# Turning the gate's rows of two chunks with one transfer, and a smaller block of zeros

## The chip, the cores and the metric

The kernel runs on one core of a Trainium2 chip. The metric is device time in microseconds (us). TensorE multiplies matrices, VectorE and ScalarE work on tiles in the on-chip memory (SBUF), GpSimd issues indirect transfers, and SyncE (SP) issues all other transfers, one after the other, from one queue. The transfers themselves run on 16 DMA engines.

## The reference, cut to what matters

Attention over 8 batches of 3072 tokens, with 256 features and keys of 64, gives `x`. A gate then sends each token to one of 8 experts (two layers, 256 to 1024 to 256); an expert takes its first 768 tokens in order, and all other tokens give zeros.

```python
scores = (1.0 / S) * np.matmul(z, z.transpose(0, 2, 1))
attn = np.maximum(scores, 0.0) ** 2
x = (u * np.matmul(attn, v)).reshape(B * S, D)
logits = x @ w_gate
expert_idx = np.argmax(logits, axis=1)
# softmax weight of the chosen expert; disp[e] = its first `capacity` tokens
h = np.maximum(np.einsum('ecd,edf->ecf', disp, w1), 0.0)
y = np.einsum('ecf,efd->ecd', h, w2)
# out[i] = gate weight * y of the token's slot, or zeros for tokens beyond capacity
```

## The kernel before, in words

Every fp32 value is split into two fp16 halves, a high and a low one, and a product is three fp16 matmuls. Attention goes by blocks of 512 queries (four chunks of 128 tokens), 14 blocks in all, since by then each expert has had its 768 tokens; the last block has two chunks only. The code after the straight part, for inputs where that is not so, is skipped here. A block takes 12 pairs of key tiles. Scores are symmetric, so scores of earlier blocks are stored (`kept`, line 942) and later loaded and turned by one transfer each (`ld`, line 858); there are 40 such loads, and five buffers of them, which TensorE gives back.

When a block's sums are done, `route` (line 648 on) runs the gate on it. The rows are scaled and split: ScalarE writes the high halves (line 666), VectorE the low halves (line 669), both into a tile `xr` with one row of 264 words (1056 bytes) for each token: 256 words that hold the two halves, four with the gate's weight (line 729), four with the token's number (line 732). A transposing transfer from SyncE's queue turns the halves of one chunk, 128x512 fp16, into `xt` (line 677): 54 of them in the kernel. TensorE makes the logits out of `xt` (line 684), four matmuls a chunk, VectorE takes the largest, counts places, and GpSimd scatters each chunk's rows into the experts' buffer `disp` (line 84).

The order of all this is written at build time by a planner: `Chain` holds stages of items with an engine and an assumed cost, and `weave` emits an item when an assumed clock of its engine allows. A transposing transfer is of the kind `XB`; line 194 moves the planned clock of SyncE on by the larger of 1.2 and 0.3 plus its cost. The gate's transfers are given 0.45 each. The stage of the gate's matmuls waits in the plan for the planned landing and then 4.5 us more (`LAG`), 0.5 in the last block.

Rows of `out` that no expert fills must be zeros. `put_zeros` (line 1253) stores a block of 512 rows, 512 KB, out of a tile of zeros with 512 columns, 48 times: 14 during the last two blocks of attention, the others while the experts run. The experts read 768 rows of `disp` at a time, turned by one transfer (`fxt`, line 1120), in two buffers.

Of the kernel before, what the change touches and what calls it, by code (L numbers as in the profile page):

```python
# [9 lines left out]
F32 = mybir.dt.float32  # L10
F16 = mybir.dt.float16
I32 = mybir.dt.int32
AF = mybir.ActivationFunctionType
# [5 lines left out]
P = 128  # L19
BLK = 512  # L20
# [6 lines left out]
def attention_moe_kernel(ctx: ExitStack, tc: tile.TileContext, u, v, z, w_gate, w1, w2, out, cap):  # L27
    nc = tc.nc
    B, S, D = u.shape
    DQ = z.shape[2]  # L30
    E = w_gate.shape[1]
# [7 lines left out]
    DC = D // P  # L39
    FC = F // P  # L40
    CAPP = -(-cap // P) * P
    ROWW = D + MROW
    SLAB = min(CAPP, 768)
    NB0 = min(NBLK, -(-(E * cap * 7) // (6 * BLK)))
    assert DQ == 64 and D == 256 and S % BLK == 0 and F % P == 0 and DC * F == 2 * 1024

    const = ctx.enter_context(tc.tile_pool(name="const", bufs=1))
# [33 lines left out]
    def scatter(key, dst, idx, src, bound):  # L81


        r = nc.gpsimd.indirect_dma_start(out=dst, out_offset=bass.IndirectOffsetOnAxis(ap=idx, axis=0), in_=src,  # L84
                                         in_offset=None, bounds_check=bound, oob_is_err=False)
        if straight[0]:
            apart(r, key, [key] + (["zeros"] if cleared[0] and key == "out" else []))
            scattered[key].append(r.ins.name)
# [16 lines left out]
    cnt = const.tile([P, E], F16, name="cnt")  # L105
    wg16 = const.tile([P, DC, 2 * E], F16, name="wg16")
    wginv = const.tile([P, 1], F32, name="wginv")
    zero = const.tile([P, 512], F32, name="zero")
    more = const.tile([1, 1], I32, name="more")
    redo = const.tile([1, 1], I32, name="redo")  # L110
    short = const.tile([1, 1], I32, name="short")
# [536 lines left out]
    def route(x, bt, after, lag, cc, rid):  # L648
# [7 lines left out]
        def r_bits():  # L656
            st.rs, inv = pow2(st.m, cc, 3, "rs")
            st.f = sm.tile([P, cc], F32, tag="rf", name="rf")
            st.fg = sm.tile([P, cc], F32, tag="rfg", name="rfg")
            ts(st.f, inv, bt.cb, ALU.mult)  # L660
            ts(st.fg, inv, bt.cbg, ALU.mult)
            st.xr = sb.tile([P, cc, ROWW], F32, tag="xr", name="xr")
            st.x16 = st.xr.bitcast(F16)

        def r_hi(c):
            return lambda: nc.scalar.activation(st.x16[:, c, 0:D], st.x[:, c, :], AF.Copy, scale=st.rs[:, c:c + 1])  # L666

        def r_lo(c):
            return lambda: nc.vector.scalar_tensor_tensor(
                out=st.x16[:, c, D:2 * D], in0=st.x[:, c, :], scalar=st.rs[:, c:c + 1], in1=st.x16[:, c, 0:D],  # L670
                op0=ALU.mult, op1=ALU.subtract)

        def r_tr(c):
            def f():
                if c == 0:
                    st.xt = sb.tile([P, cc, 2 * DC, P], F16, tag="xt", name="xt", bufs=1)
                nc.sync.dma_start_transpose(out=st.xt[:, c], in_=st.x16[:, c, 0:2 * D])
            return ("XB", 0.45, f, None)

        def r_lg():  # L680
            st.lg = ps.tile([P, cc, 2, E], F32, tag="m", name="lg", bufs=1)
            for c in range(cc):
                for q in range(2 * DC):
                    nc.tensor.matmul(st.lg[:, c].rearrange("p h e -> p (h e)"), lhsT=st.xt[:, c, q, :],  # L684
                                     rhs=wg16[:, q % DC, :], start=(c == 0 and q == 0),
                                     stop=(c == cc - 1 and q == 2 * DC - 1), skip_group_check=True)

# [30 lines left out]
        def r_exp():  # L718
            nc.scalar.activation(st.ex, st.ex, AF.Exp)

        def r_gate():
            s = sm.tile([P, cc], F32, tag="es", name="es")
            g = sm.tile([P, cc], F32, tag="eg", name="eg")
            nc.vector.tensor_reduce(out=s, in_=st.ex, axis=AX.X, op=ALU.add)
            ts(s, s, 1e-9, ALU.add)
            nc.vector.reciprocal(g, s)
            nc.vector.tensor_mul(g, g, st.f)
            meta = st.xr[:, :, D:D + 8]
            nc.vector.tensor_copy(meta[:, :, 0:4], g.unsqueeze(2).to_broadcast([P, cc, 4]))

        def r_tok():
            nc.vector.tensor_copy(st.xr[:, :, D + 4:D + 8], tokid[:, 0:cc].unsqueeze(2).to_broadcast([P, cc, 4]))
            ts(tokid, tokid, float(cc * P), ALU.add)

        def r_slot():
# [15 lines left out]
            nc.vector.tensor_add(cnt, cnt, c1)  # L751

        def r_sc(c):
            return lambda: scatter("disp", disp, st.slot[:, c:c + 1], st.xr[:, c, :], E * CAPP - 1)

        def hi(h):
            return [("ACT", 0.4, r_hi(c), None) for c in (2 * h, 2 * h + 1)]
# [2 lines left out]
            return [("DVE", 0.4, r_lo(c), None) for c in (2 * h, 2 * h + 1)]  # L760

        def tr(h):
            return [r_tr(c) for c in (2 * h, 2 * h + 1)]

        nh = cc // 2
        Chain([
# [466 lines left out]
    with tc.manual_schedule():  # L1233

        halved = NB0 >= 3 and NB0 % BPB != 1
        bats = {b: batch(b) for b in range(-(-NB0 // BPB))}
        for b, bt in bats.items():
            n = min(BPB, NB0 - b * BPB)  # L1240
            bt.follows = {(j - 1, j) for j in range(1, n)}
            for i, j in ((i, j) for j in range(n) for i in range(j - 1)):
                bt.kept[i, j] = dram.tile([BLK, 2, 2, HB], F16, name=f"kept{b}_{i}_{j}")
        b0 = bats[0]
        early = min(5 * P, CAPP)
        cuts = [(0, early - P), (early - P, P)]
        assert halved
        prepare(b0, True)
        make_consts()
        warm_up(30)  # L1250
        Chain([[("DVE", 1.2, more_consts, "consts")], [("DVE", 0.8, prep_gate, "gate")]], 4, 40.0)

        def put_zeros(i):
            def f():
                r = nc.sync.dma_start(
                    out=out[i * BLK:(i + 1) * BLK].rearrange("(q r h) d -> q r (h d)", q=P, h=2),
                    in_=zero.unsqueeze(1).to_broadcast([P, BLK // P // 2, 2 * D]))
                if i >= NB0:
                    apart(r, "zeros", ["out"])
                    cleared[0] = True  # L1260
            return ("SP", 1.46, f, ("zero", i))


        zq = deque(range(NB0))

        begun = [Bag() for _ in range(1 + len(cuts))]

        def begin(after):
            for (s0, n), sx in zip(cuts, begun[1:]):
                slab(0, s0, n, sx, after, 0)  # L1270

        def hook(p):
            n, g = divmod(p, NPAIR)
            if p == 1:
                init_disp()
            b, ib = divmod(n, BPB)
            if g == 0 and ib == (b == 0) and b + 1 in bats:
                prepare(bats[b + 1])
            if n >= (NB0 - 1) // BPB * BPB and zq:
                Chain([[put_zeros(zq.popleft())]], 4)  # L1280
            if g == 0 and n == max(NB0 - 2, (NB0 - 1) // BPB * BPB):
                weights(0, begun[0])
            if n == NB0 - 2 and g == 0:
                scs, cn = last_route[0]
                watchers.append((lambda: all(x in done for x in scs), lambda: (
                    begin(max(done[x] for x in scs)), check_early(min(early, cap), done[cn]))))

        blocks = [(bats[n // BPB], n % BPB, 0, CC if n < NB0 - 1 else CC // 2) for n in range(NB0)]
        attention(blocks, hook)
        cn = last_route[0][1]  # L1290
        watchers.append((lambda: cn in done, lambda: check_full(done[cn] + 25.0, 0)))
        need(*[("zero", i) for i in range(NB0)])
        while not all(hasattr(x, "id") for x in begun[1:]):
            weave()
            clk["PE"] += 0.1
        Chain([[put_zeros(i)] for i in range(NB0, NTOK // BLK)], 4, clk["PE"] + 5.0)
        experts(list(range(E)), begun, cuts, last_route[0][0])
        finish()

        straight[0] = False  # L1300
        flag = nc.values_load(redo, min_val=0, max_val=1)
        with tc.If(flag > 0):
            nb, ib0 = divmod(NB0, BPB)

            def tail(b, ibs, half=()):
                go_on = nc.values_load(more, min_val=0, max_val=1)
                with tc.If(go_on > 0):
                    bt = batch(b)
                    prepare(bt)
                    attention([(bt, ib, CC // 2, CC // 2) for ib in half] + [(bt, ib, 0, CC) for ib in ibs],  # L1310
                              lambda p: None)
                    finish()
                    check_full()
                    finish()

            if ib0:
                tail(nb, range(ib0, BPB), [ib0 - 1])
                nb += 1
            else:
                tail(nb - 1, [], [BPB - 1])  # L1320
            if nb < B:
                with tc.For_i(nb, B, 1) as b:
                    tail(b, range(BPB))
            with tc.For_i(0, E, 1) as e:
                experts([e])
                finish()
# [25 lines left out]
```

## Time and profile before

| what | value |
|---|---|
| median of three runs | 794.9 us (793.57 to 795.0) |
| the profiled execution's own time | 795.26 us |
| its span | 793.5 us |
| granted clock of TensorE | 0.998 of full speed |
| busy: TensorE, VectorE, ScalarE, GpSimd | 98%, 62%, 51%, 15% |
| share of 16 DMA engines, SyncE's queue | 70.3% |

A busy share is an average over the whole span. What a change is worth is read at the places where TensorE stands still, from what ended its waits. The span is a little shorter than the execution's own time, which also holds the start and the end around it.

### The profile page before, as it was taken

Reading aid. Unit: us, or ns where it says so; the run is one execution under the profiler, and the core shown is the slowest. Engines: PE = TensorE matmul, PEld = TensorE weight load, DVE = VectorE, ACT = ScalarE, POOL = GpSimd, SP = SyncE. Lnnn points to the kernel's source line nnn. Section 1 sums busy time; section 2 is a strip of 40 time slices with the busy share of each in tenths; the row PEclk is TensorE's granted clock in tenths of the full one; section 3 lists DMA queues with packets and bytes.
Section 4 is the critical chain, followed back from the end, with each engine's and each line's share of the span. In section 5 each row is a group of like instructions: output and inputs, shape, how many; then the busy total and the mean of one; then the engine's idle time right before and its main releaser. Section 6 shows DMA issues by size and latency. Waiting matters only on the chain.

```text
span 793.5 us, 16997 instructions
## 1 busy us (share of the span) xinstructions
PE 774.7 (98%) x6861; PEld 605.9 (76%) x6861; DVE 493.3 (62%) x1080; ACT 402.8 (51%) x692; POOL 117.2 (15%) x122
## 2 busy tenths in 40 slices
PE   9999999999999999999999999998999999999996
PEld 3677878788877778788888877876676876867865
DVE  6897788653527789964543369877565473464540
ACT  6985565523216757562422248564565464464541
POOL 0000011010102020201011020104121322312202
PEclk9999999999999999999999999999999999999999
DMA  7659999898977948988799949783996946824001
GB/s 219 131 202 177 246 213 222 194 219 189 197 140 169 295 141 167 270 169 185 148 233 200 194 125 235 288 196 130 249 316 243 322 127 245 257 54 144 29 15 43
DMA packets 283832, 149.53 MB, mean 188 GB/s; under 512 B 229741, under 2 KB 255674, under 8 KB 283744
## 3 DMA queue, kind: packets, MB, share of 16 engines
q1 hardware_dynamic: 278848, 135.57, 70.3%
q0 software_dynamic: 4896, 12.79, 4.7%
q8 instruction: 55, 0.90, 0.5%
q14 instruction: 33, 0.27, 0.1%
HBM read 36.25 MB, written 59.92 MB: 121 GB/s over the span
## 4 chain that ended last, share of the span: by engine, by line
PE 82%; DMA 6%; issue 4%; DVE 3%; SPq 1%; ACT 1%; POOL 1%; POOLq 0%; ACTq 0%; DVEq 0%
PE acc L1025 47%; PE hps L1164 14%; PE yps L1186 13%; PE sc L885 7%; DMA ld<-kept 3%; DMA vraw<-in_v 1%; DMA fxt<-disp 1%; POOL out L84 1%; DVE hl L911 1%; PE lg L684 1%; DVE vm L73 1%; DVE hl L920 1%; ACT a L907 0%; SPq L362 0%; ACT r L902 0%
## 5 line engine op out<-in xcount | busy, mean ns | idle before, releaser
L1025 PE MATMUL acc<-v,hl 128*128 128x256 f16 x2280 | 259.3, 273 | 0.0
L1025 PEld LDWEIGHTS <-hl 128*128 128x128 f16 x2280 | 219.9, 98 | 33.9 <-issue 4.7
L902 ACT ACTIVATE r<-sc 128x512 f32<-128x512 f32 (+1 forms) x212 | 105.5, 549 | 167.4 <-PE sc L885 161.7
L1164 PE MATMUL hps<-fxt,wt 128*128 128x384 f16 (+2 forms) x816 | 127.2, 317 | 3.0 <-DVE wt L1093 1.4
L1186 PE MATMUL yps<-wt,hh 128*128 128x256 f16 x1152 | 128.1, 273 | 1.1 <-issue 1.1
L1150 DVE SCALAR_TENSOR_TENSOR hh<-hps,hh 128x384 f16<-128x384 f32 (+2 forms) x136 | 71.5, 531 | 86.8 <-ACT hh L1149 86.0
L1186 PEld LDWEIGHTS <-hh 128*128 128x128 f16 x1152 | 112.4, 98 | 15.6 <-issue 1.6
L920 DVE TENSOR_TENSOR hl<-a,hl 128x1024 f16<-128x1024 f32 (+1 forms) x106 | 118.2, 1115 | 3.6
L1164 PEld LDWEIGHTS <-wt 128*128 128x128 f16 x816 | 75.9, 98 | 51.4 <-issue 3.5
L1025 PE MATMUL acc<-v,ld 128*128 128x256 f16 x960 | 108.2, 273 | 4.0 <-DMA ld<-kept 4.0
L84 POOL DMA_INDIRECT disp<-xr,slot x54 | 56.3, 1042 | 339.9 <-issue 159.3
L1025 PEld LDWEIGHTS <-ld 128*128 128x128 f16 x960 | 92.8, 98 | 16.8 <-DMA ld<-kept 4.9
L911 DVE CAST hl<-a 128x1024 f16<-128x1024 f32 (+1 forms) x106 | 67.8, 640 | 59.8 <-ACT a L907 59.3
L907 ACT ACTIVATE a<-r 128x1024 f32<-128x1024 f32 (+1 forms) x106 | 102.6, 968 | 2.5
L1149 ACT ACTIVATE hh<-hps 128x384 f16<-128x384 f32 (+2 forms) x136 | 63.3, 471 | 53.9 <-PE hps L1164 52.7
L885 PE MATMUL sc<-zz 64*128 64x512 f16 (+1 forms) x636 | 71.5, 356 | 1.5 <-DVE zz L424 1.4
L84 POOL DMA_INDIRECT out<-ys,sid x48 | 54.1, 1127 | 124.5 <-ACT ys L1192 73.5
L1192 ACT ACTIVATE ys<-yps,sg 128x256 f32<-128x256 f32 x48 | 22.7, 472 | 75.9 <-PE yps L1186 71.1
L1025 PE MATMUL acc<-v,nx 128*128 128x256 f16 x504 | 59.2, 273 | 0.0
L666 ACT ACTIVATE xr<-x,rsr 128x256 f16<-128x256 f32 x54 | 25.1, 502 | 59.8 <-DVE rsr L60 57.7
L1025 PEld LDWEIGHTS <-nx 128*128 128x128 f16 x504 | 48.1, 98 | 9.4 <-issue 4.0
L885 PEld LDWEIGHTS <-zz 64*128 64x128 f16 x636 | 26.9, 94 | 35.2 <-issue 11.3
(128 smaller groups left out, 460.0 us busy)
## 6 DMA issues: line engine op xcount, KB each, us to landing
out<-zero SPq DMA_DIRECT2D x48, 512.0 KB
kept<-hl SPq DMA_DIRECT2D x40, 512.0 KB
wraw<-in_moe_w SPq DMA_DIRECT2D x32, 512.0 KB
vraw<-in_v SPq DMA_DIRECT2D x18, 512.0 KB
u<-in_u SPq DMA_DIRECT2D x13, 512.0 KB
zraw<-in_z SPq DMA_DIRECT2D x2, 768.0 KB
zz<-zz SPq DMA_DIRECT2D x4, 384.0 KB
xt<-xr SPq DMA_TRANSPOSE x54
```

What stands on the lines that cost most here:

```text
L84: r = nc.gpsimd.indirect_dma_start(out=dst, out_offset=bass.IndirectOffsetOnAxis(ap=idx, axis=0), in_=src, in_offset=None, bounds_check=bo ...
L666: return lambda: nc.scalar.activation(st.x16[:, c, 0:D], st.x[:, c, :], AF.Copy, scale=st.rs[:, c:c + 1])
L885: nc.tensor.matmul(s[jj][:, 0:w], lhsT=bt.zz[rows, (kl + jj) % 2, j * P:(j + 1) * P], rhs=bt.zz[rows, (ql + jj) % 2, q0:q0 + w], start=(i ...
L902: nc.scalar.activation(sct[p][:, jj, :], s[jj][:, 0:w], AF.Relu)
L907: nc.scalar.activation(sq[p], sct.pop(p), AF.Square)
L911: nc.vector.tensor_copy(hl[:, :, :, 0, :], sq[p].rearrange("p j (t k) -> p j t k", k=HB))
L920: nc.vector.tensor_sub(hl[:, :, :, 1, :], a.rearrange("p j (t k) -> p j t k", k=HB), hl[:, :, :, 0, :])
L1025: nc.tensor.matmul(o, lhsT=a(h, jj, c), rhs=bt.v2[:, j, l], start=(j + h + l + c % 2 == 0), stop=(j == JT - 1 and h == 1), skip_group_chec ...
L1149: Chain([[("ACT", 0.05 + w * 0.00083, lambda: nc.scalar.activation(th, src, AF.Relu), None)], [("DVE", 0.07 + w * 0.00104, lambda: nc.vect ...
L1150: [("DVE", 0.07 + w * 0.00104, lambda: nc.vector.scalar_tensor_tensor(out=tl, in0=src, scalar=0.0, in1=th, op0=ALU.max, op1=ALU.subtract), ...
L1164: nc.tensor.matmul(o, lhsT=wx.w1[:, d, wp, f * P:(f + 1) * P], rhs=sx.xt[:, xp * DC + d, a:a + w], start=(q == 0), stop=(q == len(seq) - 1))
L1186: nc.tensor.matmul(y, lhsT=hid(i, f)[:, sl], rhs=w[:, l], start=(f + i + l == 0), stop=(f == FC - 1 and i == 1))
```

## The change

The rows of two neighbouring chunks now lie in one piece of the tile: the first at word 0, the second at word 320 (`XR`), so that both start at a multiple of 128 fp16 columns. One transfer turns columns 0 to 1151 of the piece, nine times 128 (`NX`): four of the first chunk, one with the first chunk's weight, number and the gap, four of the second. Its planned cost is 0.9. The gap up to word 320 is filled by the token copy, which writes words 256 to 319 of the first chunk with the token's number; the gate's weight then overwrites four of these. Each of the two copies is now two instructions. The tile of zeros has 128 columns instead of 512, and each store of zeros reads it in pieces of 128 words (512 bytes), where it read pieces of 512 words.

```diff
+    XR = -(-2 * ROWW // P) * P // 2
+    NX = 2 * XR // P + 2 * DC
...
-    zero = const.tile([P, 512], F32, name="zero")
+    zero = const.tile([P, 128], F32, name="zero")
...
-            st.xr = sb.tile([P, cc, ROWW], F32, tag="xr", name="xr")
-            st.x16 = st.xr.bitcast(F16)
+            st.xr = sb.tile([P, cc // 2, XR + ROWW], F32, tag="xr", name="xr")
+
+        def xr(c):
+            return st.xr[:, c // 2, c % 2 * XR:c % 2 * XR + ROWW]
...
-        def r_tr(c):
+        def r_tr(h):
             def f():
-                if c == 0:
-                    st.xt = sb.tile([P, cc, 2 * DC, P], F16, tag="xt", name="xt", bufs=1)
-                nc.sync.dma_start_transpose(out=st.xt[:, c], in_=st.x16[:, c, 0:2 * D])
-            return ("XB", 0.45, f, None)
+                if h == 0:
+                    st.xt = sb.tile([P, cc // 2, NX, P], F16, tag="xt", name="xt", bufs=1)
+                nc.sync.dma_start_transpose(out=st.xt[:, h], in_=st.xr.bitcast(F16)[:, h, 0:NX * P])
+            return ("XB", 0.9, f, None)
...
+        def put(val, spans):
+            for k, (a, b) in enumerate(spans):
+                nc.vector.tensor_copy(st.xr[:, :, a:b], val.rearrange("p (h k) -> p h k", k=2)[:, :, k:k + 1]
+                                      .to_broadcast([P, cc // 2, b - a]))
...
-            meta = st.xr[:, :, D:D + 8]
-            nc.vector.tensor_copy(meta[:, :, 0:4], g.unsqueeze(2).to_broadcast([P, cc, 4]))
+            put(g, ((D, D + 4), (XR + D, XR + D + 4)))
...
-            nc.vector.tensor_copy(st.xr[:, :, D + 4:D + 8], tokid[:, 0:cc].unsqueeze(2).to_broadcast([P, cc, 4]))
+            put(tokid[:, 0:cc], ((D, XR), (XR + D + 4, XR + D + 8)))
...
         def tr(h):
-            return [r_tr(c) for c in (2 * h, 2 * h + 1)]
+            return [r_tr(h)]
...
-                    out=out[i * BLK:(i + 1) * BLK].rearrange("(q r h) d -> q r (h d)", q=P, h=2),
-                    in_=zero.unsqueeze(1).to_broadcast([P, BLK // P // 2, 2 * D]))
+                    out=out[i * BLK:(i + 1) * BLK].rearrange("(q r) (h d) -> q (r h) d", q=P, h=2),
+                    in_=zero.unsqueeze(1).to_broadcast([P, 2 * BLK // P, D // 2]))
```

## Rows read from the trace of the kernel before

**Rows 1.** The page, busy us (share of the span) and instructions of each engine.
```profile
PE 774.7 (98%) x6861; PEld 605.9 (76%) x6861; DVE 493.3 (62%) x1080; ACT 402.8 (51%) x692; POOL 117.2 (15%) x122
```

**Rows 2.** What TensorE waited for: us in total, times, longest us.
```profile
PE acc L1025 <- DMA ld<-kept: 4.0, 3, 1.5
...
PE hps L1164 <- DMA fxt<-disp: 0.5, 1, 0.5
```

**Rows 3.** Tile xt: duration ns min/median/max of an issue; idle ahead of it (us, times).
```profile
L677 SPq DMA_TRANSPOSE xt<-xr x54: 1189/1215/2285, 70.9 to 538.6; - x54
...
  DMA xt<-xr: 0.2, 1
```

**Rows 4.** What SyncE's queue waited for, the same columns as rows 2.
```profile
SPq L677 <- DVE xr L669: 29.2, 6, 10.4
```

**Rows 5.** Tiles nx and zero, the same columns as rows 3.
```profile
L935 SPq DMA_TRANSPOSE nx<-hl x44: 1232/1322/5179, 29.6 to 482.3; - x44
...
L119 POOL MEMSET zero<- x1: 525/525/525, 0.7 to 0.7; 128x512 f32 x1
```

**Rows 6.** Timeline of SyncE's queue, three stretches: start us, us, engine, line, operation.
```profile
222.69 2.53 SPq L677 DMA_TRANSPOSE xt<-xr  x2
225.31 1.88 SPq L858 DMA_TRANSPOSE ld<-kept  x1
...
302.33 2.54 SPq L677 DMA_TRANSPOSE xt<-xr  x2
...
557.11 1.23 SPq L1255 DMA_DIRECT2D out<-zero  x2
...
558.65 5.40 SPq L1120 DMA_TRANSPOSE fxt<-disp  x1
```

**Rows 7.** Timeline of TensorE around 231 and 567.
```profile
210.37 13.26 PE L1025 MATMUL acc<-v,ld 128*128 128x256 f16 x120
...
231.19 1.16 PE L1025 MATMUL acc<-v,ld 128*128 128x256 f16 x9 [1.14 <-DMA ld<-kept]
...
567.14 1.62 PE L1164 MATMUL hps<-fxt,wt 128*128 128x384 f16 x9 [0.55 <-DMA fxt<-disp]
```

**Rows 8.** The chain that ended last, four places: start us, us, what.
```profile
140.83 7.70 DMA ld<-kept
...
221.02 1.57 SPq L858
...
222.69 1.22 SPq L677
...
312.34 1.23 DVE hl L920
...
317.78 9.63 DMA ld<-kept
...
414.13 2.42 DMA xt<-xr
```

**Rows 9.** Stretches: us, busy PE, PEld, DVE, ACT, POOL, clock, DMA share, GB/s.
```profile
637.00:646.00 9.00, 9.00 (x59) 5.58 (x58) 6.91 (x12) 6.49 (x14) 0.31 (x1) 1.00 0.05 16
588.50:590.00 1.50, 1.50 (x16) 1.34 (x15) 1.31 (x2) 0.23 (x1) 1.00 (x1) 1.00 1.27 290
628.00:632.00 4.00, 4.00 (x32) 2.96 (x31) 0.50 (x1) 1.01 (x3) 0.98 (x1) 1.00 1.05 408
2.50:3.50 1.00, 1.00 (x4) 0.30 (x2) 0.82 (x8) 0.00 (x0) 0.00 (x0) 1.00 1.15 346
144.00:147.00 3.00, 3.00 (x29) 2.51 (x26) 1.90 (x4) 3.00 (x7) 0.00 (x0) 1.00 1.23 266
300.00:320.00 20.00, 20.00 (x198) 16.13 (x196) 19.04 (x32) 13.46 (x19) 0.81 (x1) 1.00 0.91 184
```

**Rows 10.** VectorE's groups, shapes apart: busy us, mean ns of one, idle us before.
```profile
L732 DVE COPY xr<-tokid 128x16 f32<-128x16 f32 x13 | 2.3, 174 | 14.9 <-ACT xr L666 14.9
...
L302 DVE COPY dinit<-tslot 128x192 f32<-128x192 f32 x1 | 0.3, 252 | 0.0
```

More of the change, by code (lines that the diff above doesn't have):

```diff
@@ L661, in r_bits, with x16 @@
             ts(st.fg, inv, bt.cbg, ALU.mult)
-            st.xr = sb.tile([P, cc, ROWW], F32, tag="xr", name="xr")
-            st.x16 = st.xr.bitcast(F16)
+            st.xr = sb.tile([P, cc // 2, XR + ROWW], F32, tag="xr", name="xr")
+        def xr(c):
+            return st.xr[:, c // 2, c % 2 * XR:c % 2 * XR + ROWW]
+        def x16(c, a):
+            return xr(c).bitcast(F16)[:, a:a + D]
         def r_hi(c):
-            return lambda: nc.scalar.activation(st.x16[:, c, 0:D], st.x[:, c, :], AF.Copy, scale=st.rs[:, c:c + 1])
+            return lambda: nc.scalar.activation(x16(c, 0), st.x[:, c, :], AF.Copy, scale=st.rs[:, c:c + 1])
         def r_lo(c):
             return lambda: nc.vector.scalar_tensor_tensor(
-                out=st.x16[:, c, D:2 * D], in0=st.x[:, c, :], scalar=st.rs[:, c:c + 1], in1=st.x16[:, c, 0:D],
+                out=x16(c, D), in0=st.x[:, c, :], scalar=st.rs[:, c:c + 1], in1=x16(c, 0),
                 op0=ALU.mult, op1=ALU.subtract)
-        def r_tr(c):
+        def r_tr(h):
             def f():
-                if c == 0:
-                    st.xt = sb.tile([P, cc, 2 * DC, P], F16, tag="xt", name="xt", bufs=1)
-                nc.sync.dma_start_transpose(out=st.xt[:, c], in_=st.x16[:, c, 0:2 * D])
-            return ("XB", 0.45, f, None)
+                if h == 0:
+                    st.xt = sb.tile([P, cc // 2, NX, P], F16, tag="xt", name="xt", bufs=1)
+                nc.sync.dma_start_transpose(out=st.xt[:, h], in_=st.xr.bitcast(F16)[:, h, 0:NX * P])
+            return ("XB", 0.9, f, None)
         def r_lg():
@@ L683, in r_lg @@
                 for q in range(2 * DC):
-                    nc.tensor.matmul(st.lg[:, c].rearrange("p h e -> p (h e)"), lhsT=st.xt[:, c, q, :],
+                    nc.tensor.matmul(st.lg[:, c].rearrange("p h e -> p (h e)"), lhsT=st.xt[:, c // 2, c % 2 * (NX - 2 * DC) + q, :],
                                      rhs=wg16[:, q % DC, :], start=(c == 0 and q == 0),
@@ L753, in r_sc @@
         def r_sc(c):
-            return lambda: scatter("disp", disp, st.slot[:, c:c + 1], st.xr[:, c, :], E * CAPP - 1)
+            return lambda: scatter("disp", disp, st.slot[:, c:c + 1], xr(c), E * CAPP - 1)
         def hi(h):
```

## The prediction

> **What bounds the kernel now.** I read the page's table of engines first, then the list of what TensorE waits for, then its instructions around each wait, and last the chain of waits and SyncE's queue ahead of them. The table shows TensorE busy for 774.7 of 793.5 us [rows 1]. The change leaves its instructions as they are: the same 216 gate matmuls on other slices of one tile. So only its idle time, 18.8 us, can move, and much of that is not reachable: the first scores wait for the first loads, and after the last matmul there is a tail of scatters. What the change can touch is in the list of waits [rows 2]: 4.0 us in three waits for transfers of kept scores (`ld`), 0.5 us for an expert's rows (`fxt`). Its waits for gate rows come to only 0.2 us, in one place [rows 3]. So the gate's own transfers are hidden almost everywhere; what they can do is hold up other things on the same queue.
>
> **The gate's transfer, issue.** Two transfers of 128x512 become one of 128x1152: 54 issues become 27. A 128x512 issue took 1189 ns at least and 1215 in the median, one of 128x1024 (`nx`) 1232 and 1322 [rows 3, 5]. So the issue hardly grows with the size: I take 1.24 us, and each pair frees about 1.27 us of SyncE's queue, 27 x 1.27 = 34 us in all. That pays only where the queue is the step that TensorE waits for. I go through the three waits.
>
> At 231.19 it is. Ahead of the late load (issued at 225.31) two gate transfers stand back to back from 222.69 [rows 6], and the chain goes through them [rows 8]. The load ahead of them started its transfer when TensorE gave a buffer back at 221.02 [rows 8]; the next buffer follows one kept piece later, 24 matmuls of 0.11 us (13.26/120), at about 223.7 [rows 7]. With one transfer from 222.69, SyncE is free at about 224.0, after the buffer. The load starts 1.27 us sooner and the wait was 1.14 [rows 7]: minus 1.14 us. The bound on the other side is nothing gained, if the larger transfer ahead takes from the load on the DMA engines what the queue gave.
>
> At 148.57 it is not. That load was issued at 140.83, just when TensorE stopped needing its buffer, and landed 7.70 us later [rows 8]; the DMA engines are full then (share 1.23 from 144 to 147) [rows 9]. The gate's transfers lie 25 us earlier. Nothing. At 327.45 it is not either: the chain to it runs through VectorE (`hl`, 312.34) and then the stores of kept scores [rows 8]; the gate's transfers ended at 304.9 [rows 6]. Nothing from the queue.
>
> The gate's own wait: the last of four transfers in a row at 414.13 landed after 2.42 us and the gate matmuls waited 0.2 us at most [rows 3, 8]. The second joined one ends some 1.3 us sooner. Minus 0.1 us. For the other blocks the planner leaves 4.5 us before the gate matmuls, and it now counts on the landing 0.75 us earlier (one 0.9 behind one issue, instead of 0.45 behind two); 2.42 us plus the longer transfer still fits. The joined transfer also waits for both chunks' low halves before it starts, 0.48 us more of a held queue where SyncE waits for VectorE (six waits [rows 4]); it gives back 1.27 at once.
>
> **The gate's transfer, bytes.** Nine pieces of 128 columns instead of eight: 32 KB more for each pair. Transfers of this kind alone moved 290 GB/s [rows 9], so 0.11 us a pair, 0.23 us a block, 3 us over the kernel. It counts only where a load waits on full DMA engines: two of the three waits, 0 to 0.5 us together; I take nothing, since no gate transfer lies in the 8 us before either.
>
> **VectorE.** The token copy writes 128 elements a partition and then 8, instead of 16; the gate copy becomes two of 8. A 16-element copy took 174 ns and one of 192 elements 252 [rows 10], so the wide copy is about 224: plus 0.05 + 0.17 + 0.17 = 0.4 us for a block of four chunks. VectorE is busy 493.3 of 793.5 us [rows 1] and hides it mostly. The token copy fills the gap that the transfer reads, so the transfer waits for it too; it stands ahead of the low halves on VectorE, and these come last. The gate copy writes columns that the transfer has read, and comes out of its result anyway. Only the chain to 327.45 has it on the path: 19.04 of 20 us busy from 300 to 320 [rows 9]. The token copy of that block comes ahead of it, the gate copy after: plus 0.2 us, bounds 0 and 0.4.
>
> **The block of zeros.** 48 stores of 512 KB are cut into pieces of 512 B instead of 2 KB. With 2 KB pieces they ran alone at 408 GB/s, 1.28 us each [rows 9]. No store of 512 B pieces is in the trace; the nearest row is the first load of `z`, which moves such pieces: 346 GB/s [rows 9], 1.52 us. The other end is the 290 GB/s of transposing transfers, 1.81 us. So 0 to 0.53 us more each; I take 0.24. In the expert stage the DMA engines stand nearly still for some 9 us of each expert's 31 (share 0.05 from 637 to 646) [rows 9], which hides six of them. One place is bare: two stores of zeros issued at 557.11 are right ahead of the `fxt` transfer of 558.65, and TensorE waited 0.55 us for that at 567.14 [rows 6, 7]. Plus 0.5 us, bounds 0 and 1.1. The clearing of the smaller block on GpSimd (0.5 us at the start [rows 5]) is waited for by nobody.
> The Trainium skill (DMA: Bandwidth & Descriptors, Specifications) puts full rate at pieces of 512 B and up, so by it the zeros cost nothing and the sum would be 0.5 us lower; the row with 346 GB/s speaks against it, but that row reads from HBM, so no row here settles it.
>
> **Sum.** -1.14 - 0.1 + 0.2 + 0.5 = -0.5 us against the profiled execution's own 795.26 us (span 793.5 and 1.8 around it): 794.7. That execution was 0.36 above the median of the three runs, so against the median 794.9 I say 794.4. With all bounds it is 793.6 (no wait at 231, none for gate rows, nothing added) to 796.9 (nothing gained, 0.5 + 0.4 + 1.1 added); the order that the planner writes also shifts, because its clock of SyncE runs 1.2 us less ahead after each pair, and that may move single loads by some tenths. Its own range: 793.0 to 796.9.
>
> **Rivals.** (1) The plan gains more. With SyncE's planned clock shorter, loads and stores are issued sooner and all waits for transfers go: 4.0 + 0.5 + 0.2 [rows 2, 3] = 4.7, so 790.2; half of it 792.5. For: the queue's freed 34 us. Against: two of the three waits have other causes. (2) It gets slower: a kept load that stands right behind a joined transfer finds 288 KB ahead of it instead of 128 KB, 160 KB at 290 GB/s or 0.55 us, in stretches where the DMA engines have no air (1.23). There are 40 kept loads in eight blocks; if the wait at 231 stays and two more loads become late by the mean of the three, 1.33 us, with the zeros at 1.1: 794.9 + 2.7 + 1.1 + 0.2 = 798.9; with one more and the zeros as taken, 796.9. It decides from loads that now land within half a microsecond of their use. For: three loads are late already. Against: the queue gives 1.27 back for each 0.55. (3) The joined transfer doesn't save an issue: its odd ninth piece makes it cost two. Then nothing is gained and the rest is added: 795.6. Against it: 128x1024 issues at 1322 ns.
>
> **Chances.** A measurement of this kernel can tell about 0.2% (1.6 us) from no change. The forecast's case 0.5, the faster rival 0.25, the slower 0.17, the third 0.08. Of the forecast's case a little lies below 793.3 and a little above 796.5, and of the faster rival a part stays within. Together: faster 0.30, same 0.49, slower 0.21. The range leaves out the outer parts of both rivals: 791.2 to 797.2.
>
> **What would show it.** Right: 27 transfers of the gate with issue times near 1.24 us; no wait at the load that now ends at 231; a wait for `fxt` near 567 of about 1 us; zeros moving near 350 GB/s; TensorE's busy time unchanged. Wrong: a new wait for kept loads elsewhere, an issue near 2.4 us, or a shift in the stage from 540 to 570, where attention passes over to the experts, if the planner orders it anew.

## The result, and the profile after

The change made the kernel slower: 800.37 us in the median of 12 runs, 794.95 for the kernel before beside it, ratio 1.0064 [1.0049, 1.0078]. A second comparison gave 797.49 against 794.78, ratio 1.0032 [1.0017, 1.0048]. I had said 794.4 and 791.2 to 797.2. The profiled execution took 801.72 us (span 799.9), 6.4 more span than before.

The page's engines:

```profile
PE 779.0 (97%) x6861; PEld 607.1 (76%) x6861; DVE 495.6 (62%) x1108; ACT 402.5 (50%) x692; POOL 121.9 (15%) x122
```

What TensorE waited for (us in total, times, longest):

```profile
PE acc L1038 <- DMA ld<-kept: 3.6, 3, 2.1
PE lg L691 <- DMA xt<-xr: 2.4, 4, 1.0
PE hps L1177 <- DMA fxt<-disp: 2.1, 1, 2.1
```

Against [rows 1, 2] the number of matmuls is the same, but they are busy for 4.3 us more. There are again three waits for kept loads, the gate's own waits have grown from 0.2 to 2.4 us, and that for `fxt` from 0.5 to 2.1. Tiles `xt` and `zero`, issue times as in [rows 3, 5]:

```profile
L684 SPq DMA_TRANSPOSE xt<-xr x27: 1268/1319/3077, 71.9 to 541.4; - x27
...
L1268 SPq DMA_DIRECT2D out<-zero x48: 548/1634/4119, 474.9 to 694.0; - x48
```

A joined transfer costs one issue, 1319 ns against 1215, so the saving itself is there: 54 x 1.215 - 27 x 1.319 = 30 us of SyncE's queue. A store of zeros now takes 1634 ns to issue in the median, 804 before. TensorE's timeline, at the places where it lost time (start, us, engine, line, operation, idle before):

```profile
139.49 2.79 PE L1038 MATMUL acc<-v,ld 128*128 128x256 f16 x24 [0.78 <-DMA ld<-kept]
...
146.85 2.79 PE L1038 MATMUL acc<-v,ld 128*128 128x256 f16 x24 [0.76 <-DMA ld<-kept]
151.69 4.04 PE L1038 MATMUL acc<-v,ld 128*128 128x256 f16 x24 [2.05 <-DMA ld<-kept]
155.53 3.24 PE L1038 MATMUL acc<-v,nx 128*128 128x256 f16 x24
...
195.98 0.36 PE L691 MATMUL lg<-wg,xt 128*128 128x16 f16 x8 [0.99 <-DMA xt<-xr]
...
496.23 0.36 PE L691 MATMUL lg<-wg,xt 128*128 128x16 f16 x8 [0.97 <-DMA xt<-xr]
...
572.05 10.62 PE L1177 MATMUL hps<-fxt,wt 128*128 128x384 f16 x54 [2.10 <-DMA fxt<-disp]
```

The wait at 231 [rows 7] and the one at 327 are gone; others stand in their place. And 24 matmuls that take 2.79 us took 4.04 and 3.24 right after the wait of 2.05. The windows there (engines busy, then granted clock, DMA share, GB/s):

```profile
150.00:160.00 10.00, 8.31 (x60) 5.90 (x60) 4.16 (x7) 0.49 (x2) 0.00 (x0) 0.83 0.95 184
570.00:580.00 10.00, 7.95 (x39) 4.37 (x39) 2.79 (x5) 3.15 (x7) 1.95 (x2) 0.83 1.12 282
...
629.00:639.00 10.00, 10.00 (x87) 8.19 (x85) 1.75 (x2) 2.63 (x6) 3.44 (x3) 1.00 1.08 343
```

0.83 over 10 us is some 3.4 us at the lower of the clock's two levels (1.2 instead of 2.4 GHz), each time right behind a wait of two microseconds. Each such stretch costs 1.25 + 0.45 = 1.7 us (the two rows of 24 behind that wait, 4.04 and 3.24, against 2.79). The two of them are 3.4 of the 4.3 us that TensorE is busy for longer.

The n-th matmul after set against the n-th before shows where the 6.4 us arise (roughly, since the order differs in places): +4.8 up to 158 (start and kept loads, 1.7 of it clock), +1.35 at 193, -1.3 at 234, +0.4 up to 320, -1.2 at 327, +1.2 at 491 (gate rows, as at 193), -1.8 from 552 to 562, +3.2 from 567 to 577 (`fxt`, 1.7 of it clock).

### The profile page after: what moved, and what is told of

The parts are those of the page before. It is cut to its first block, busy times and chain, and to the rows that moved or that the text cites. A ratio compares the mean times of both kernels' runs of the same rounds, so it can differ in the third digit from the quotient of the medians.

```text
span 799.9 us, 16952 instructions
## 1 busy us (share of the span) xinstructions
PE 779.0 (97%) x6861; PEld 607.1 (76%) x6861; DVE 495.6 (62%) x1108; ACT 402.5 (50%) x692; POOL 121.9 (15%) x122
## 4 chain that ended last, share of the span: by engine, by line
PE 80%; DMA 6%; DVE 6%; issue 4%; ACT 2%; POOL 1%; SPq 0%; another core or an unknown queue 0%; POOLq 0%; ACTq 0%; DVEq 0%
PE acc L1038 48%; PE hps L1177 12%; PE yps L1199 12%; PE sc L898 8%; DMA ld<-kept 2%; DMA xt<-xr 2%; DMA vraw<-in_v 1%; DMA fxt<-disp 1%; POOL out L86 1%; ACT r L915 1%; PE lg L691 1%; DVE hh L1163 1%; DVE wt L1106 1%; DVE wm L75 1%; ACT a L920 1%
## 5 line engine op out<-in xcount | busy, mean ns | idle before, releaser
L86 POOL DMA_INDIRECT disp<-xr,slot x54 | 62.4, 1156 | 374.3 <-DVE xr L732 193.6
```

## The experiments

**What each part is worth.** Planned cost, transfer and zeros can be had apart. In e1 only the zeros are changed. In e2 both transfers stay, but are planned as one item of 0.9, which puts SyncE's queue and TensorE in the order of the changed kernel. In e3 and e4 the joined transfer is planned as two items of 0.45, which puts both in the order of the kernel before; e3 keeps the zeros' 2 KB pieces. In the cuts, `...` stands for lines left out.

```diff
# e2
...
-                nc.sync.dma_start_transpose(out=st.xt[:, c], in_=st.x16[:, c, 0:2 * D])
-            return ("XB", 0.45, f, None)
+                for c in (2 * h, 2 * h + 1):
+                    nc.sync.dma_start_transpose(out=st.xt[:, c], in_=st.x16[:, c, 0:2 * D])
+            return ("XB", 0.9, f, None)
...
# e3, e4, e15 (from the changed kernel)
-            return ("XB", 0.9, f, None)
+            return [("XB", 0.45, f, None), ("XB", 0.45, lambda: None, None)]
...
# e3, e7, e8, e12, e14: zeros of 2 KB
...
+                    zero.append(sb.tile([P, 512], F32, tag="zraw", name="zero", bufs=1))
+                    nc.gpsimd.memset(zero[0], 0.0)
...
```

> The kernel before with only its block of zeros cut to 128 columns, so that the 48 stores go in pieces of 512 bytes; the order of all instructions is the one before. Theory Z (the zeros): the stores hold the DMA engines longer just ahead of the experts' rows, the wait there grows from 0.55 to about 2.1 us and a stretch of TensorE's lower clock follows, so 2 to 4 us slower than before. Theory P (the order the planner writes) and theory T (the joined transfer lands later): within 1 us of before. By the prediction's own step: 0.5 us slower.

> The kernel before, with two transfers for a pair of chunks as before, but planned as one item of 0.9, so that all queues stand in the order of the changed kernel. Theory P: the new order alone costs most of it, 3 to 5 us slower than before, with new waits for kept loads near 140 to 152 and waits of the gate's matmuls. Theories Z and T: within 1 us of before.

> The joined transfer and its tile, but planned as two items of 0.45 (the second issues nothing), so that all queues stand in the order before; zeros in pieces of 2 KB, from a tile in the space of the raw z. Theory T: 2 to 4 us slower than before, with waits of the gate's matmuls for the transfer. Theories P and Z: as before or up to 1.5 us faster, with the wait at 231 gone, as the prediction's first step has it.

> The whole change (joined transfer, zeros in pieces of 512 bytes) in the order before: the joined transfer is planned as two items of 0.45. Theory P: the loss of the change is gone but for the zeros, 0 to 1.5 us slower than before. Theory Z: 2 to 4 us slower. Theory T: 2 to 4 us slower. If two theories hold in part, this run and the changed kernel differ by what the order alone costs.

Before beside them: 795.71. e1 798.72, ratio 1.0032 [1.0017, 1.0047]; e2 807.99, 1.0157 [1.0134, 1.0181]; e3 791.45, 0.9948 [0.9931, 0.9965]; e4 791.95, 0.9957 [0.9941, 0.9972]. So the transfer gains about 4 us, and the order that the planner writes loses 12 alone. No expectation had the gain (for e4 I had at best no loss, for e3 up to 1.5 us), and the loss of e2 was put at 3 to 5. The two don't add up: with the joined transfer the order costs 800.37 - 791.95 = 8.4 us, and by the second comparison's ratio some 6 to 7 (1.0032 against 0.9957 in e4 and 0.9942 in e15). Where both sides have zeros of 2 KB it costs 4 to 6 (1.0000 in e7 and 1.0019 in e12, both below, against 0.9948 in e3). What TensorE waited for in e2, then in e4:

```profile
PE lg L685 <- DMA xt<-xr: 5.1, 8, 1.0
PE acc L1026 <- DMA ld<-kept: 5.0, 7, 1.7
```

```profile
PE hps L1177 <- DVE wt L1106: 1.7, 1, 1.7
...
PE hps L1177 <- DMA fxt<-disp: 0.6, 1, 0.6
```

In e4 no wait for a kept load or a gate row is left: those at 148 and 327 went too, which I had said the queue couldn't reach.

**Is it the issues, or the new tile?** e8 has the old order, the new tile and its copies, but turns the nine pieces by two transfers, five and four.

```diff
-                nc.sync.dma_start_transpose(out=st.xt[:, h], in_=st.xr.bitcast(F16)[:, h, 0:NX * P])
...
+                nc.sync.dma_start_transpose(out=st.xt[:, h, 0:5], in_=st.xr.bitcast(F16)[:, h, 0:5 * P])
...
+                nc.sync.dma_start_transpose(out=st.xt[:, h, 5:NX], in_=st.xr.bitcast(F16)[:, h, 5 * P:NX * P])
...
```

> The new tile, the two extra copies of VectorE, the nine pieces and the old order, with zeros of 2 KB, but each pair turned by two transfers again, of five and of four pieces. If the 4.3 us that the joined transfer gains in the old order come from the freed issues: 795 to 797, with the three waits for kept loads back. If they come from the layout or the bytes: 790.5 to 792.5.

796.83, ratio 1.0006 [0.9975, 1.0037]. The waits for kept loads are back:

```profile
PE acc L1039 <- DMA ld<-kept: 3.7, 4, 2.2
```

With the new tile and its bytes, but without the freed issues, the gain is gone. So the gain is that of the freed issues.

**Which side of the new plan: SyncE's queue, or the earlier gate matmuls?** e5 has the new clock of SyncE and the old landing, e6 the old clock and the new landing.

```diff
# both, in Chain.emit
-                self.late = max(self.late, t)
+                self.late = max(self.late, t + slip.pop() if slip else t)
# e5, in r_tr: the landing as if planned as two
+                slip.append(max(clk["DMA"] - 0.45, clk["SP"] + 1.4) + 0.45 - clk["DMA"])
# e6: two items of 0.45, the landing as if planned as one
...
+                slip.append(0.45)
+            return [("XB", 0.45, f, None), ("XB", 0.45, lambda: slip.append(-10.0), None)]
...
```

> The whole change, planned as made except that the landing of the joined transfer, for which the gate's matmuls wait in the plan, is counted as late as that of two transfers was. SyncE's planned clock stays short, so its queue keeps most of the new order of loads and stores, and the gate's matmuls stand late again. Theory G (what costs is the gate's matmuls standing 0.75 us earlier): 792 to 794, near the change in the old order, 791.95. Theory Q (what costs is the new order of loads and stores in SyncE's queue): 797 to 801, with waits for kept loads near 140 to 152 as in the changed kernel and none for the gate.

> The counterpart: the whole change with SyncE's clock planned as before (two issues), and only the landing counted early, as in the change as made. SyncE's queue keeps the old order but for one short stretch, and the gate's matmuls stand 0.75 us earlier. Theory G: 796 to 800, with four or more waits of the gate's matmuls of about 1 us. Theory Q: 791 to 794.

e5 798.7, ratio 1.0047 [1.0025, 1.0069]; e6 791.3, 0.9954 [0.9934, 0.9974]. In e6 the gate matmuls stand earlier and wait for nothing; e5 has one wait of 0.9 us for gate rows, where I expected none. By what stands at each place of SyncE's queue, e5 has the changed kernel's order up to 257 us and other shifts behind, e6 the old order but for seven places near 300. It is the queue's order.

**Which stretch, and which item.** e9 keeps the old plan for the first three blocks and takes the new one behind, e10 the other way round. e13 holds three loads of `v` in the changed kernel back to their old planned times. e16, e17 and e18 take the new plan for the gate of one block alone, the first, second or third.

```diff
# e9 (e10: nth >= 3; e16, e17, e18: nth != 0, 1, 2)
-            return ("XB", 0.9, f, None)
+            return [("XB", 0.45, f, None), ("XB", 0.45, lambda: None, None)] if nth < 3 else [("XB", 0.9, f, None)]
...
# e13
+        held = {3: 89.3, 4: 94.0, 5: 100.9}
...
-                Chain([[("SP", 1.46, ld_v(i), None)], [mark(i)]], 2, slow=20.0)
+                Chain([[("SP", 1.46, ld_v(i), None)], [mark(i)]], 2, held.get(i, 0.0) if isinstance(bt.b, int) and bt.b == 1 else 0.0, slow=20.0)
```

> The whole change; the first three blocks' transfers are planned as before (two items of 0.45), the rest as made. So the queues stand in the old order through the first 150 us and in the new one after. If the new order costs in the first stretch, where it brings loads of v ahead: 792 to 795. If it costs in the later stretches: 797 to 801. By the changed kernel's trace I expect 1 us of gate waits near 491 and the place near 570 to remain: 794 to 796.

> The counterpart: the first three blocks planned as made, the rest as before. If the new order costs in the first stretch: 796 to 799, with waits for kept loads of 3 us and more between 137 and 152; if later: 791 to 793.

> The change as made, but the last three loads of v for the second batch are held back in the plan until the times that they have in the old order (89.3, 94.0 and 100.9 of the plan instead of 82.7, 87.1 and 89.7). The transfers of the gate and of z then stand in SyncE's queue as before through 150 us; the rest is the new order. If the loads of v that slip ahead cost the first stretch: 792 to 795, like the kernel whose first three blocks are planned as before (793.8), and the waits near 137 to 152 go. If something else in the new order does: 796 to 799.

> The change with the planner's old accounting everywhere but at the first block's gate, which has the new one. SyncE's queue then stands up to 130 us as in the kernel that has the new accounting in its first three blocks (v's loads one place earlier, xt x2 ahead of zz, u behind nx), and in the old order afterwards. Theory (what costs in the first stretch is set by the first block's shift: the loads of v and the turn of the batch's new z): 1.0015 of before, kept loads waited for near 146 to 151, 1.5 to 2.5 us. Rival (it is the second or third block's own shift): 0.995, no such wait.

> The same with the new accounting at the second block's gate alone. The loads of v and the order of xt and zz stay as before; the two stores of zz are moved from behind the kept loads to between the nx transfers and the first kept stores. Theory (v and the turn of z cost, the stores of zz don't): 0.995, at most 1 us of waits for kept loads. Rival (the stores of zz, 384 KB each, put ahead of the kept loads are what costs): 1.001, waits for kept loads near 140 to 151.

> The same with the new accounting at the third block's gate alone: SyncE's order is the old one throughout, and only 108 lines of TensorE's order differ, gate matmuls of that block that stand earlier among the others. Both theories: 0.995, with at most one wait for gate rows of about 1 us. If it were the gate matmuls' place that costs, 0.998 or more.

e9 793.77, 0.9989 [0.9972, 1.0006]; e10 796.58, 1.0019 [1.0002, 1.0036], both against 794.78; the old order throughout stands at 0.994 to 0.996. So the first three blocks cost about 5 us and the others about 3; the gate waits, 3.8 us in five places in e9 and none in e10, belong to the latter. e13 came to 798.38, 1.0025 [1.0004, 1.0046]: my theory that the earlier loads of `v` do it was not borne out. Of the last three, beside the kernel before (797.17): e18 791.65, 0.9937 [0.9916, 0.9959]; e16 796.66, 0.9986 [0.9968, 1.0003]; e17 795.91, 0.9986 [0.9971, 1.0001]. Against e18 the first block's shift costs 0.5%, and the second's, which I had expected to cost nothing, as much. The third's costs nothing that can be seen: in e18 SyncE's queue stands in the old order. SyncE's queue from 110 to 148 (start, us, engine, line, operation), e4 first, then e18, then the kernel before:

```profile
111.60 1.26 SPq L460 DMA_TRANSPOSE zz<-zhl  x1
...
127.10 6.96 SPq L871 DMA_TRANSPOSE ld<-kept  x2
...
138.26 4.08 SPq L871 DMA_TRANSPOSE ld<-kept  x1
```

```profile
111.10 1.30 SPq L688 DMA_TRANSPOSE xt<-xr  x1
...
140.06 3.74 SPq L875 DMA_TRANSPOSE ld<-kept  x1
```

```profile
113.27 2.53 SPq L677 DMA_TRANSPOSE xt<-xr  x2
...
128.99 7.38 SPq L858 DMA_TRANSPOSE ld<-kept  x2
...
140.83 3.93 SPq L858 DMA_TRANSPOSE ld<-kept  x1
```

The changed kernel, then e16, then e17, which shares its order with e13 from 114 on:

```profile
111.87 2.73 SPq L684 DMA_TRANSPOSE xt<-xr  x2
114.69 5.95 SPq L460 DMA_TRANSPOSE zz<-zhl  x2
...
130.55 8.59 SPq L871 DMA_TRANSPOSE ld<-kept  x2
...
144.68 2.96 SPq L871 DMA_TRANSPOSE ld<-kept  x1
```

```profile
114.17 5.07 SPq L460 DMA_TRANSPOSE zz<-zhl  x2
...
129.67 8.74 SPq L875 DMA_TRANSPOSE ld<-kept  x2
...
143.80 4.02 SPq L875 DMA_TRANSPOSE ld<-kept  x1
```

```profile
121.72 0.52 SPq L468 DMA_DIRECT2D zz<-zz  x1
...
127.72 0.48 SPq L468 DMA_DIRECT2D zz<-zz  x1
...
129.53 9.35 SPq L875 DMA_TRANSPOSE ld<-kept  x2
...
143.56 2.97 SPq L875 DMA_TRANSPOSE ld<-kept  x1
```

Between `xt` and the last of the four kept loads no two entries of these lists lie more than 0.2 us apart. TensorE needs that last load at some 147 to 150. What became of it:

| kernel | its issue starts | and ends | TensorE waits for it, us |
|---|---|---|---|
| e4 | 138.3 | 142.3 | 0 |
| e18 | 140.1 | 143.8 | no wait listed |
| before | 140.8 | 144.8 | 1.50 |
| e17 | 143.6 | 146.5 | 1.89 |
| e16 | 143.8 | 147.8 | 1.53, and 1.98 for the load ahead of it |
| after the change | 144.7 | 147.6 | 2.05 |

The items differ, the effect is one: what the plan puts ahead of the kept loads delays them. In e16 and after the change it is the turn of the next batch's `z`, which now stands in the queue and waits there for VectorE (two in 5 to 6 us, where e4 does one in 1.26). SyncE's waits for it between 104 and 150 us, after the change and then in e4 (us, times, longest):

```profile
SPq L460 <- DVE zhl L456: 2.5, 1, 2.5
```

```profile
SPq L460 <- DVE zhl L456: 0.3, 1, 0.3
```

So the queue is not full of work there: after the change one entry holds all those behind it while its rows are not ready. In e17 it is the two stores of `zz`, 0.52 + 0.48 us of issue and 768 KB, by estimate 1.9 us at the 408 GB/s of [rows 9]. e13 has these ahead of the loads as well, so holding back `v` brought in another delay, and e13 doesn't tell what the loads of `v` cost by themselves:

```profile
121.33 0.52 SPq L468 DMA_DIRECT2D zz<-zz  x1
...
127.41 0.48 SPq L468 DMA_DIRECT2D zz<-zz  x1
...
129.24 9.30 SPq L872 DMA_TRANSPOSE ld<-kept  x2
```

The issue of two kept loads is longer too (6.96 us in e4, 9.35 in e17, 8.59 after the change). How much of this is bytes that are still moving and how much a buffer that TensorE still holds was not taken apart.

**The zeros in the change.** e7 and e12 are the changed kernel with 2 KB pieces, e11 the changed kernel again beside e12.

> The change as made, in its new order, with zeros stored in pieces of 2 KB, from a tile in the space of the raw z. If the zeros cost in the changed kernel what they cost alone (0.3%): 797 to 798.5 against its 800.4, the wait near 570 back to about 0.5 us. If they cost what they cost in the old order (0.5 us): 799.5 to 800.5.

> The changed kernel itself, beside its parts on the same chip: 799 to 802. It is there to be compared with the next one.

> The change as made with zeros in pieces of 2 KB, again, now beside the changed kernel on the same chip. If the zeros cost 6 us in the new order, as two separate comparisons gave (800.4 and 794.3): 794 to 796 against some 800. If that was the chip: within 3 us of the changed kernel.

e7 794.31, 1.0000 [0.9977, 1.0023]; e11 797.49, 1.0032 [1.0017, 1.0048]; e12 795.97, 1.0019 [1.0005, 1.0034]. Beside each other the small pieces cost 1.5 us in the median, with overlapping intervals; the 6 us between 800.37 and e7 came from two comparisons and can't be read so. The first transfers of the expert stage, lines of TensorE's and then of SyncE's timeline, in e11 and below it in e12, last TensorE's line in e1:

```profile
566.91 10.62 PE L1177 MATMUL hps<-fxt,wt 128*128 128x384 f16 x54 [3.12 <-DMA fxt<-disp]
...
555.76 2.96 SPq L1268 DMA_DIRECT2D out<-zero  x2
558.83 4.94 SPq L1133 DMA_TRANSPOSE fxt<-disp  x1
```

```profile
566.55 8.94 PE L1175 MATMUL hps<-fxt,wt 128*128 128x384 f16 x54 [1.73 <-DMA fxt<-disp]
...
556.79 2.05 SPq L1271 DMA_DIRECT2D out<-zero  x2
558.94 4.54 SPq L1131 DMA_TRANSPOSE fxt<-disp  x1
```

```profile
568.60 10.62 PE L1164 MATMUL hps<-fxt,wt 128*128 128x384 f16 x54 [1.95 <-DMA fxt<-disp]
```

Two stores of zeros ahead of `fxt` hold the queue for 2.96 us with small pieces, 2.05 with large ones in e12 and 1.23 before [rows 6]. In the profile of the changed kernel that heads this document they held it for 2.10 with small pieces, so the pieces alone don't set it. The same 54 matmuls take 8.94 us in one and 10.62 in the other, whose clock is the lower one for a part: 1.68 us on top of the wait.

**The best of it.** e14 is e6 with 2 KB zeros, e15 is e4 again.

> A version made of the parts that gained: joined transfer, SyncE's clock planned as for two issues, landing planned early, zeros in pieces of 2 KB. If zeros of 512 bytes cost 0.5 us and more there: 789.5 to 791.5, the fastest; if not, as without that, 791 to 792.

> The whole change in the old order again, beside the two others on the same chip: 791 to 793, about 4 us under the kernel before.

e14 791.65, 0.9951 [0.9934, 0.9968]; e15 791.94, 0.9942 [0.9922, 0.9963], both against 796.38. The change with SyncE's queue in the old order beats the kernel before by 0.4 to 0.6%, three times over (e4, e15, e18). With that order the pieces of the zeros make no difference that can be seen (e3 to e4 0.5 us; e6 and e14 0.9954 and 0.9951), and e14 was not the fastest, as I had thought it might be.

## Why the prediction was wrong

**The order (the step that failed).** I had written that the planner's shifted order "may move single loads by some tenths", and gave that no term of the sum. The issue of the last kept load near 140 ends 2.9 us later than before and 5.3 later than in e4. The order costs some 6 to 8 us with the joined transfer (e4 and e15 against the two timings of the change), 12 without it (e2). The shift of 1.2 us in the planned clock was in the text. What I didn't do is follow it to the place where nothing in SyncE's queue can slip without the kept loads slipping too. With a clock that runs 1.2 us less ahead after each pair, the planner puts other entries (the turn of `z`, the stores of `zz`) ahead of those loads.

**"Only its idle time, 18.8 us, can move".** Wrong as well: TensorE was busy for 4.3 us more, 3.4 of it in two stretches at the lower clock behind waits.

**148 and 327: "Nothing from the queue".** Wrong; both waits went in e3, e4, e15 and e18. I read the last releaser in the chain (a buffer that TensorE gave back, VectorE's `hl` [rows 8]) and left it there. But SyncE's queue is back to back from 109 to 145 ahead of the one: two issues saved at 110 to 115 bring the load's issue forward by 140.83 - 138.26 = 2.57 us, 25 us later. In e18 it starts only 0.77 us sooner, since the first gate transfer itself starts 1.75 later there (111.10 against 109.35), and that was enough. At 327 the queue is back to back as well from 296 on, and the issue of the kept loads starts at 313.84 in e4 instead of 317.78; that this is the cause there was not tested by itself, and in e14 0.8 us of that wait is left.

**231: -1.14.** Right as to mechanism and size: the wait is gone in e4, in the old order, and 0.66 us of it is back in e8, where only the issues are two again. It is gone after the change too, but there the queue's order had changed as well, so that the changed kernel alone would not have shown it.

**The gate's own wait: -0.1, "2.42 us plus the longer transfer still fits".** Right with the old queue (e6: no such wait though the landing is planned early), wrong with the new one (2.4 us in four waits after, 3.8 in five in e9), since the transfers start later there.

**The sum of issues.** 34 us said, 30 measured; 1.24 us an issue said, 1.319 measured. The third rival (two issues for one) is out. The larger transfer's bytes, put at nothing, cost nothing that shows: e4 moves them and no load is late.

**VectorE.** 5.6 us of busy time over 14 blocks said, 2.3 found (495.6 against 493.3); in e4 no wait of TensorE is put down to the two copies.

**Zeros: +0.5, bounds 0 and 1.1.** The place was right, the size too small for the case with the lower clock: e1 has 1.95 us of wait and the same 10.62 us for 54 matmuls, ratio 1.0032, 2.5 us. The rate was right, 343 GB/s in the window above, where I had taken 346, the load of `z` [rows 9]. That window and the one with 408 GB/s hold other transfers besides the zeros; where the stores of zeros alone moved, it was 347 with small pieces (e1, 582 to 588) and 406 with large ones (before, 580.5 to 584). What I left out is that stores behind one another hold SyncE's queue for longer, 1634 against 804 ns in the median.

The Trainium skill (DMA: Bandwidth & Descriptors, Specifications) gives 512 B as the least size for full rate; here pieces of 512 B moved at 347 GB/s and pieces of 2 KB at 406, so the trace does not bear out full rate from 512 B on, and the measurement decides.

**The rivals.** The first one's gain can be had (791.9 in e4 and e15 against its 790.2 to 792.5), but by the freed issues and with the old planned clock; the shorter planned clock, which I had named as its cause, is what loses it. The second one's sign came true, but not its mechanism: e4 has the larger transfer ahead of the kept loads, and no load is late. All cases of "slower" had 0.21, and a loss by the planner's order was none of the rivals.

## What to carry to other kernels

When a planner writes the order, a changed cost is a change of its own: make the edit once with the old planned costs, so that the order stays, and judge the two apart. A queue that stands back to back can hand a saved issue on to an entry much later (25 us here), whatever the chain names as the releaser there; so look for the next gap in the queue before a saving is set to nothing. A third of a per cent between two comparisons of one kernel (1.0064 and 1.0032 here) is a reason to time variants beside each other.

## What the runs showed of the hardware

The granted clock fell to its lower level for about 3.4 us behind some of TensorE's waits, at 1.7 us each. It did after single waits of 1.95 (e1), 2.03 (e10), 2.05 and 2.10 us (after the change), after all six of 2.91 to 3.75 us (e5, e6, e8, e9, e10, e11), and after waits of 1 to 1.9 us with others close by (e2, e3, e4, e15). It did not after 1.73 (e12), 1.98 (e16, where the next 24 matmuls took 2.79 us), 2.13 (e13), 2.20 (e8), 2.22 (e2) or 2.42 us (e5). So between 1.95 and 2.42 us the wait's length alone doesn't decide, and what does is open. The fast kernels e3, e4 and e15 have one such stretch each, so the clock is not what sets the orders apart.

The issue of a transposing transfer hardly depends on its size: 1215 ns for 128x512, 1319 for 128x1152 (medians).

A plain store of 512 KB took 552 to 569 ns to issue when it was the first of its group in the expert stage, whether in 256 pieces of 2 KB or in four times as many (the kernel before and after the change). The median of all 48 was 804 and 1634 ns. So what grew with the number of pieces is the issue of stores that follow others.
